# Attention with routed experts on one core: the steps ahead of the first expert in a new order, its first token block copied alone, more dummy products

## The chip, the cores and the metric

The kernel runs on one core of a Trainium2 chip. The metric is the device time of one execution in microseconds. The core has five engines with queues of their own: TensorE (PE: matrix products and transposes; its weight loads are listed as PEld), VectorE (DVE), ScalarE (ACT), GpSimd (POOL) and SyncE (SP, which here only issues DMAs). The engines wait for each other by semaphores. Products land in PSUM, everything else lies in SBUF.

## The reference

A causal attention over 8 batches, 12 heads, 448 positions and 64 columns a head is followed by a layer of 8 experts. Each of the 8 x 448 = 3584 tokens has 768 columns; each expert takes at most 80 tokens.

```
x = attention(q, k, v)                      # 3584 tokens x 768
logits = x @ w_gate                         # 8 experts
expert_idx = argmax(logits);  gate_w = softmax(logits)[expert_idx]
for e in range(8):
    tok_idx = tokens whose expert is e, the 80 with the largest gate_w
    h = maximum(x[tok_idx] @ w1[e], 0)      # 768 -> 1024
    out[tok_idx] = gate_w[tok_idx] * (h @ w2[e])   # 1024 -> 768
```

Rows of `out` that no expert took are zero.

## The kernel before, in words

**Attention** runs over the batches and, in each, over six pairs of heads. A plan in slots says which piece of which step is issued when. After the attention of a batch its tokens are written to the buffer `xs` in device memory, and a table of the 80 best tokens of every expert is brought up to date: tokens of the batch are compared with each other and with those already in the table.

**The tail** is this work for the last batch. Nothing is left to hide it in, so its order is written out by hand in the string `TAIL` (L43 to L48). Every word is a step; `tc.manual_schedule()` (L974) keeps the steps in this order on every engine. The words that matter here:

- `r0` to `r7`: the eight groups of rows of the last batch (two groups of columns times four blocks of tokens). `w` is the turn on TensorE (three transposes, `rt`, L592), `e` takes it out of PSUM and `m` multiplies by the softmax's norm. `ROW_ENGINES` (L49) names who does it: `v` is one VectorE instruction; `a` is six ScalarE multiplications (L605); `p` is one ScalarE copy (L607) at `e` and a GpSimd multiplication (L619) at `m`. Each group ends with a store to `xs`, issued by SP (L615).
- `r0t r0c`, `r1t r1c`: the one-hot rows and the weights are transposed (`selt`, L731) and copied to `ex` by ScalarE (L734). `hold` is a GpSimd copy (L721) behind which `r1t` is issued.
- `rl lt cp ro`: products of the old table's row with the new tokens (`rl`, L761), comparisons on VectorE (`lt`, L767), counts on TensorE (`cp`, L774) and new ranks on VectorE (`ro`, L779). `places` and `places_more` turn the ranks into two halves of a one-hot table (`rm`, L794).
- `c3w c3l` to `c0w c0l`: the tokens of the batch against each other, a product `rn` (L745) and a VectorE comparison `less` (L748) for each block; `gt3` to `gt0` add them up on TensorE (L813).
- `own rank rr tn tab`: the ranks become a table (`tn`, L857, L860) and the table becomes the list of tokens `idx` (L910, L915).
- `*n`: n dummy products of 448 columns (`keep_warm`, L1096 to L1100), whose result nobody reads.

**The experts.** `gather` (L1183) reads an expert's 80 rows of `xs` by an indirect DMA that GpSimd issues. `inputs` (L1194) turns them (`xtp`, L1204) into six blocks of 128 columns and copies these out of PSUM: a float16 part `xh` on ScalarE (L1208) and the rest `xl` on VectorE (L1209). The weights are loaded in pieces of 1.5 MB and split the same way into `wh` (ScalarE, L1172) and `wl` (VectorE, L1157); a product is then three float16 products (L1230 to L1233). Some weight blocks are not split: `whole` (L1133) names blocks 3 to 5 of the first matrix of expert 0, block 5 of that of experts 1 to 5, and one of the second matrix. For these the tokens are copied in float32 as `xw` (L1207), and the product is one float32 product (L1223), which the profile lists as two passes. Expert 0 begins with its three whole blocks (L1341).

In this part only TensorE's order is fixed by hand (L1334). The program gives ScalarE eight weight splits (three blocks of expert 0 and five of expert 1) ahead of the first `xw`; splits of VectorE are issued behind the list of tokens, and later ones behind `xl`, with `issue_after` (L1156). Layer 1 of an expert is followed by layer 2 of the one before.

Of the kernel before, what the change touches and what calls it, by code (L numbers as in the profile page):

```python
# [7 lines left out]
F32 = mybir.dt.float32  # L8
# [4 lines left out]
AF = mybir.ActivationFunctionType  # L13
ALU = mybir.AluOpType
# [3 lines left out]
P = 128  # L18
# [23 lines left out]

TAIL = """  # L43
u ta ya tb yb v0 td yd tc yc v1 vy guard invert last_rows w gp0 wy close piece gp1 gs
r0w r0e r1w lp r1e r1m r2w r2e rest rest r3w r3e lg logit shifted chosen rest rest r4w r4e r5w *2
sums one_hot wsum one_zero wmore columns r0t r0c *2 weight weighted parts hold r1t r1c rl r3m r4m r5e r5m r6w r6e r6m
lt c3w c3l cp c2w r7w r7e r7m ro c2l c1w gt3 *1 c0w c1l gt2 *1 c0l *1 gt1 places *1 earlier gt0 places_more own *3 rank rr tn tab *17
"""  # L48
ROW_ENGINES = "vpappppp"  # L49


@with_exitstack
def attention_then_moe(
# [12 lines left out]
    nc = tc.nc  # L66
# [7 lines left out]
    NC1 = D // P  # L74
# [12 lines left out]
    ps_m = ctx.enter_context(tc.tile_pool(name="ps_m", bufs=2, space=PSUM))  # L87
# [30 lines left out]
    SL = max(2, min(P, CAP))  # L118
# [65 lines left out]
    wmore = [wearly]  # L184
# [19 lines left out]
    def piece_parts():  # L204

        got = []
        k = PIECES[len(wload)][3]
        got.append(piece())
        half = PW // k // 2

        def part(j, x):
            t, src = got[0]
            nc.sync.dma_start(t[:, j, x * half:(x + 1) * half], src[:, j, x * half:(x + 1) * half])
        return [lambda j=j, x=x: part(j, x) for j in range(k) for x in range(2)]
# [7 lines left out]
    lg = keep.tile([P, NT, H * E], F32, name="lg")  # L222
# [717 lines left out]
    n = len(pairs)  # L940
# [33 lines left out]
    with tc.manual_schedule():  # L974
# [14 lines left out]
            out=nowhere, out_offset=None, in_=w2.rearrange("e p c (g d) -> (e p c g) d", d=DH)[0:N, :],  # L989
# [10 lines left out]
        deferred, parts = [], []  # L1000
        for i, pr in enumerate(pairs):
# [8 lines left out]
            h = i // PH  # L1010
# [12 lines left out]
            for k in range(SLOTS):  # L1023
# [24 lines left out]
                if i > 4 and k % 4 == 3:  # L1048
                    if not parts and len(wload) < WBUF:
                        parts = piece_parts()  # L1050
# [10 lines left out]
        rest = [f for k in sorted(plan) for f in plan.pop(k)]  # L1061
# [34 lines left out]
        def keep_warm(times):  # L1096

            wp = ps_v.tile([P, S], F32, name="wp", tag="xp")
            for _ in range(times):
                nc.tensor.matmul(wp, identb, before[:, 0:S], start=True, stop=True)  # L1100
        for i, x in enumerate(ROW_ENGINES):
            g, t = divmod(i, NT)
# [25 lines left out]
    ps = ctx.enter_context(tc.tile_pool(name="ps", bufs=2, space=PSUM, reuse_waits="tile"))  # L1128
# [4 lines left out]
    def whole(e, which, c):  # L1133

        if e >= E - 2:
            return False
        return c == NC2 - 1 if which == 2 else c >= (NC1 // 2 if e == 0 else NC1 - 1)

    SW, SX = 32.0, 8.0
# [3 lines left out]
    PER = NC1 if NC1 * SL <= 512 else NC1 // 2  # L1143
# [50 lines left out]
    def inputs(u):  # L1194

        h = ffn.tile([P, NC1, SL], F16, name="xh", tag="xh")
        l = ffn.tile([P, NC1, SL], F16, name="xl", tag="xl")
        nw = sum(whole(u.e, 1, c) for c in range(NC1))
        w = ffn.tile([P, NC1 // 2, SL], F32, name="xw", tag="xw", bufs=1)
        per = NC1 // 2 if u.e == 0 else PER  # L1200
        for c0 in reversed(range(0, NC1, per)):
            tp = ps_m.tile([P, per, SL], F32, name="xtp", tag="misc", padded_shape=[P, PER, SL])
            for c in range(per):
                nc.tensor.transpose(tp[:, c, :], u.xg[:, (c0 + c) * P:(c0 + c + 1) * P], ident[0:SL, 0:SL])  # L1204
            part = slice(c0, c0 + per)
            if nw and c0 + per == NC1:
                nc.scalar.activation(w[:, NC1 // 2 - nw:], tp[:, per - nw:], AF.Copy, scale=SX * SW)  # L1207
            nc.scalar.activation(h[:, part], tp, AF.Copy, scale=SX)  # L1208
            u.xl = nc.vector.scalar_tensor_tensor(out=l[:, part], in0=tp, scalar=SX, in1=h[:, part], op0=ALU.mult,  # L1209
                                                  op1=ALU.subtract)  # L1210
        u.x = h, l, w

    def product(u, a, which, x, n, outs, per, blocks=None):
# [104 lines left out]
    for s in range(NSL):  # L1318
# [4 lines left out]
        for e in range(E):  # L1323
            u = Unit()
# [9 lines left out]
        with tc.manual_schedule(engines={mybir.EngineType.PE}):  # L1334
            for e in range(E + 1):
                if e < E:
                    u = units[e]
                    if e == 0:

                        order, lows = split_pieces(n1)  # L1340
                        u.order = order[NC1 // 2:] + order[:NC1 // 2]  # L1341
                        units[1].order, more = split_pieces(n1)
                        for nx in units[1:AHEAD]:
                            gather(nx)
                        for _, f in lows:
                            low_after.append(f())
                        inputs(u)
                        low_after.append(u.xl)
                        for _, f in more:
                            f()  # L1350
                    elif e > 1:
                        u.order = split_now(n1)
                    if e + AHEAD < E:
                        gather(units[e + AHEAD])

                    def between(p=prev, nx=units[e + 1] if e + 1 < E else None):
                        if p and p.e:
                            outputs(units[p.e - 1])
                        elif nx and not p:
                            inputs(nx)  # L1360
                    if prev:
                        hidden(prev)
                    layer1(u, between)
                if prev:
                    prev.order = split_now(n2)
                    if e == E:
                        hidden(prev)

                    between = None
                    if e + 1 < E:  # L1370
                        between = lambda u=units[e + 1]: inputs(u)
                    elif e == E and prev.e:
                        between = lambda u=units[prev.e - 1]: outputs(u)
                    layer2(prev, between)
                    if e == E:
                        outputs(prev)
# [38 lines left out]
```

## Time and profile before

| | |
|---|---|
| timed runs, median of 3 | 472.5 us (471.6 to 473.13) |
| profiled execution | 476.79 us |
| its span (first to last instruction) | 474.9 us |
| TensorE, VectorE, ScalarE, GpSimd busy | 442.5, 414.9, 397.6, 317.1 us |
| mean granted clock of TensorE | 0.988 |
| read and written | 253 GB/s over the span |
| tail of the last batch | about 330 to 348 us of the span |
| first gather issued | 348.34 us |
| last instruction of the experts on VectorE | 469.0 us |

All times of single instructions count from the start of the span. A row of the timeline gives start, length, engine, line, operation, output and inputs, shape, count, and in brackets how long the engine had stood idle before it and what ended that. A row of a stretch gives busy time and count of each engine in it, then the clock that TensorE was granted, the share of the DMA engines that were busy, and GB/s. Instructions of one engine can overlap by a little, since the next one starts before the last has written its end.

### The profile page before, as it was taken

The page shows a single profiled execution, that of the slowest core. Times are in us where ns is not written, and L with a number is a line of the kernel's source. Part 1 is how long each engine was busy: PE and PEld are TensorE (multiplying, and loading weights), DVE is VectorE, ACT ScalarE, POOL GpSimd, SP SyncE. Part 2 cuts the span into 40 slices and gives each one's busy share as a digit, 9 for nine tenths or more (in the row PEclk, how much of TensorE's full clock was granted, in tenths as well). Part 3 has the DMA queues.
Part 4 walks back from the last instruction along what each step waited for, and adds up shares of the span by engine and source line. Part 5 has one row for each costly group of instructions (what it writes and reads, how often), then busy time and mean ns, then how long its engine had stood idle before and what let it go on. Part 6 is the DMA issues. An engine that isn't in the chain of part 4 may idle for free.

```text
span 474.9 us, 14808 instructions
## 1 busy us (share of the span) xinstructions
PE 442.5 (93%) x5279; PEld 347.1 (73%) x5279; DVE 414.9 (87%) x1272; ACT 397.6 (84%) x1076; POOL 317.1 (67%) x382
## 2 busy tenths in 40 slices
PE   4899999999999999999999999999889999989894
PEld 2566677767767776776677668666569998988894
DVE  6788799988988999998899899996786999999982
ACT  6898989979988897998898889787593989988892
POOL 7999999988998996997898799720440265500101
PEclk9999999999999999999999999999996999999999
DMA  7858999899779569687956947469849999999801
GB/s 211 185 151 233 277 310 243 258 285 258 212 220 296 165 211 303 167 244 219 310 156 215 304 154 226 146 213 385 343 155 344 355 397 383 392 425 424 338 24 43
DMA packets 43001, 120.88 MB, mean 255 GB/s; under 512 B 6146, under 2 KB 23810, under 8 KB 39472
## 3 DMA queue, kind: packets, MB, share of 16 engines
q1 hardware_dynamic: 41712, 116.21, 75.7%
q0 software_dynamic: 1056, 3.51, 2.3%
q8 instruction: 41, 0.67, 0.6%
q10 hardware_dynamic: 160, 0.23, 0.2%
q14 instruction: 32, 0.26, 0.2%
HBM read 96.36 MB, written 23.99 MB: 253 GB/s over the span
## 4 chain that ended last, share of the span: by engine, by line
PE 77%; DMA 9%; DVE 7%; issue 3%; POOL 2%; SPq 1%; ACT 0%; POOLq 0%; ACTq 0%; DVEq 0%
PE xp L495 15%; PE tp L465 14%; PE sp L423 6%; DMA qk<-k_t 6%; PE sp L424 5%; PE rt L592 4%; PE hp L1223 4%; PE sp L433 3%; PE hp L1232 3%; PE hp L1233 3%; PE hp L1230 3%; PE gp L545 3%; PE op L1233 2%; PE op L1232 2%; PE op L1230 2%
## 5 line engine op out<-in xcount | busy, mean ns | idle before, releaser
L448 ACT ACTIVATE prob<-ns,nb 128x128 f32<-128x128 f32 (+3 forms) x336 | 177.2, 529 | 24.9 <-DVE nb L445 23.2
L445 DVE CUSTOM_DVE_ANT_0 ns<-sp,mask 128x384 f32<-128x384 f32 (+2 forms) x288 | 115.4, 413 | 17.9 <-PE sp L424 12.1
L465 PE MATMUL tp<-ident,prob 128*128 128x128 f32 x768 | 118.9, 277 | 1.4 <-ACT prob L448 1.2
L477 ACT COPY PT<-tp 128x512 f32<-128x512 f32 x182 | 104.0, 572 | 16.5 <-PE sp L423 7.9
L395 POOL TENSOR_TENSOR qk<-qk,qk 128x448 f16<-128x448 f32 x92 | 98.3, 1091 | 11.9 <-DVE qk L387 6.8
L1157 DVE SCALAR_TENSOR_TENSOR wl<-wraw,wh 128x768 f16<-128x768 f32 (+1 forms) x98 | 98.1, 1059 | 3.3 <-ACT wh L1172 2.2
L465 PEld LDWEIGHTS tp<-ident,prob 128*128 128x128 f32 x768 | 89.8, 142 | 13.3 <-ACT prob L448 3.3
L495 PE MATMUL xp<-PT,vt 128*64 128x448 f32 (+3 forms) x768 | 91.1, 380 | 0.0
L1172 ACT ACTIVATE wh<-wraw 128x768 f16<-128x768 f32 (+1 forms) x98 | 84.7, 926 | 3.7 <-PE hp L1233 1.2
L423 PE MATMUL sp<-qk 128*128 128x384 f16 (+2 forms) x288 | 75.9, 279 | 12.4 <-DVE nb L445 6.9
L495 PEld LDWEIGHTS xp<-PT,vt 128*64 128x64 f32 x768 | 53.8, 137 | 42.7 <-issue 22.6
L424 PE MATMUL sp<-qk 128*128 128x384 f16 (+2 forms) x288 | 78.0, 277 | 1.3 <-POOL qk L349 0.5
L1233 PEld LDWEIGHTS <-wl 128*128 128x128 f16 x668 | 67.1, 100 | 3.0 <-issue 1.5
L1232 PEld LDWEIGHTS <-wh 128*128 128x128 f16 x668 | 67.1, 100 | 2.7 <-issue 2.6
L1230 PEld LDWEIGHTS <-wh 128*128 128x128 f16 x668 | 67.6, 101 | 0.6 <-issue 0.6
L1311 POOL DMA_INDIRECT out<-yo,idx x8 | 22.4, 2802 | 66.6 <-ACT yo L1308 63.4
L448 ACT ACTIVATION_READ_ACCUMULATOR prob<-ns,nb 128x1 f32 x336 | 63.9, 190 | 0.0
L390 POOL TENSOR_TENSOR qk<-qk,qk 64x448 f16<-64x448 f32 x46 | 53.4, 1160 | 3.4
L391 POOL TENSOR_TENSOR qk<-qk,qk 64x448 f16<-64x448 f32 x46 | 51.4, 1117 | 3.2
L387 DVE CAST qk<-qk 128x896 f16<-128x896 f32 x46 | 40.0, 869 | 2.2 <-DMA qk<-k_t 2.1
L384 POOL CAST qk<-qk 64x896 f16<-64x896 f32 x40 | 38.5, 962 | 3.8 <-PE sp L436 2.5
L423 PEld LDWEIGHTS <-qk 128*128 128x128 f16 x288 | 28.5, 99 | 15.7 <-issue 7.3
(188 smaller groups left out, 905.9 us busy)
## 6 DMA issues: line engine op xcount, KB each, us to landing
wraw<-w SPq DMA_DIRECT2D x27, 1536.0 KB, 10.9
qk<-k_t SPq DMA_DIRECT2D x92, 224.0 KB, 6.0
out<-mask_l SPq DMA_DIRECT2D x56, 192.0 KB, 4.4
qk<-q_t SPq DMA_DIRECT2D x23, 448.0 KB, 4.0
vt<-v_t SPq DMA_DIRECT2D x24, 384.0 KB, 5.7
xs<-xr SPq DMA_DIRECT2D x42, 192.0 KB, 3.1
wraw<-w SPq DMA_DIRECT2D x24, 256.0 KB, 5.7
vt<-v_t SPq DMA_DIRECT2D x24, 64.0 KB, 5.2
```

Of the source, the lines that this page charges most:

```text
L395: nc.gpsimd.tensor_tensor(out=k_lo[j][:, i], in0=kf[j][:, i], in1=k_hi[j][:, i], op=ALU.subtract)
L423: nc.tensor.matmul(sp[:, 0:w], qx[:, p, t * P:w], kx[:, p, 0:w], start=True, stop=False)
L424: nc.tensor.matmul(sp[:, 0:w], qx[:, p, t * P:w], lx[:, p, 0:w], start=False, stop=True)
L445: pr.masked = nc.vector.tensor_tensor_reduce(out=ns[:, 0:w], in0=sp[:, 0:w], in1=m, scale=-1.0 / 8.0, scalar=HUGE, op0=ALU.add, op1=ALU.mi ...
L448: nc.scalar.activation(pr.P[:, off:off + w], ns[:, 0:w], AF.Exp, bias=nb, scale=-1.0, accum_out=total)
L465: nc.tensor.transpose(pr.tp[:, i], pr.P[:, off:off + P], ident)
L477: copy(dst, src)
L495: state["pe"] = nc.tensor.matmul(xp[rows, 0:w], st["vt"][:, c, p * P + j * DH:p * P + (j + 1) * DH], pr.PT[:, j, n0:n0 + w], start=(c == 0 ...
L1157: return nc.vector.scalar_tensor_tensor(out=l, in0=src, scalar=SW, in1=h, op0=ALU.mult, op1=ALU.subtract)
L1230: nc.tensor.matmul(o, wh[:, ws], ah[:, c, :], start=(x == 0 and i % per == 0), stop=False, skip_group_check=True)
L1232: nc.tensor.matmul(o, wh[:, ws], al[:, c, :], start=False, stop=False, skip_group_check=True)
L1233: nc.tensor.matmul(o, wl[:, ws], ah[:, c, :], start=False, stop=(x == n - 1), skip_group_check=True)
```

## The change

Three places are edited.

1. `TAIL`: `rl` stands ahead of `r1t`, and `lt cp ro places` stand ahead of `c3w c3l`, where `places` stood far behind. The row groups are spread anew: `r2m` and `r3m` stand earlier, `r4e`, `r4m`, `r5w` and `r5e` later. There are six more dummy products: 34 instead of 28, three of them in the last group, behind `tab` (20 instead of 17), and two ahead of `rank` (5 instead of 3).
2. `ROW_ENGINES`: row group 2 goes from `a` to `p`, row group 5 from `p` to `a`.
3. `inputs`: a block that is only used whole is no longer split into `xh` and `xl` as well. For expert 0 the six blocks are turned and copied in three parts: block 3 alone, in a PSUM tile of its own from the pool of the outputs (`ps`, tag `o`), then blocks 4 and 5, then blocks 0 to 2. Before, it was two parts of three blocks. For experts 1 to 5 `xh` and `xl` have five blocks instead of six.

```
-r0w r0e r1w lp r1e r1m r2w r2e rest rest r3w r3e lg logit shifted chosen rest rest r4w r4e r5w *2
-sums one_hot wsum one_zero wmore columns r0t r0c *2 weight weighted parts hold r1t r1c rl r3m r4m r5e r5m r6w r6e r6m
-lt c3w c3l cp c2w r7w r7e r7m ro c2l c1w gt3 *1 c0w c1l gt2 *1 c0l *1 gt1 places *1 earlier gt0 places_more own *3 rank rr tn tab *17
+r0w r0e r1w lp r1e r1m rest rest r2w r2e r2m r3w lg logit shifted r3e chosen rest rest r4w *1
+sums one_hot wsum one_zero wmore r3m columns r0t r0c *3 weight weighted parts hold rl r1t r1c *1 lt cp ro places r5w
+c3w c3l r4e r4m r5e r6w r6e r6m c2w r7w r7e r7m c2l c1w gt3 *2 c0w c1l gt2 *1 c0l gt1 *1 places_more earlier gt0
+own *5 rank rr tn tab *20
 """
-ROW_ENGINES = "vpappppp"
+ROW_ENGINES = "vppppapp"
...
-        nw = sum(whole(u.e, 1, c) for c in range(NC1))
         w = ffn.tile([P, NC1 // 2, SL], F32, name="xw", tag="xw", bufs=1)
-        per = NC1 // 2 if u.e == 0 else PER
-        for c0 in reversed(range(0, NC1, per)):
-            tp = ps_m.tile([P, per, SL], F32, name="xtp", tag="misc", padded_shape=[P, PER, SL])
-            for c in range(per):
+        parts = [(0, NC1)] if u.e else [(NC1 // 2, NC1 // 2 + 1), (NC1 // 2 + 1, NC1), (0, NC1 // 2)]
+        for i, (c0, c1) in enumerate(parts):
+            n = c1 - c0
+            if i == 0 and len(parts) > 1:
+                tp = ps.tile([P, n, SL], F32, name="xtp", tag="o", padded_shape=[P, PER, SL])
+            else:
+                tp = ps_m.tile([P, n, SL], F32, name="xtp", tag="misc", padded_shape=[P, PER, SL])
+            for c in range(n):
                 nc.tensor.transpose(tp[:, c, :], u.xg[:, (c0 + c) * P:(c0 + c + 1) * P], ident[0:SL, 0:SL])
-            part = slice(c0, c0 + per)
-            if nw and c0 + per == NC1:
-                nc.scalar.activation(w[:, NC1 // 2 - nw:], tp[:, per - nw:], AF.Copy, scale=SX * SW)
-            nc.scalar.activation(h[:, part], tp, AF.Copy, scale=SX)
-            u.xl = nc.vector.scalar_tensor_tensor(out=l[:, part], in0=tp, scalar=SX, in1=h[:, part], op0=ALU.mult,
-                                                  op1=ALU.subtract)
+            split = [c for c in range(c0, c1) if not whole(u.e, 1, c)]
+            m = len(split)
+            assert split == list(range(c0, c0 + m))
+            if m < n:
+                nc.scalar.activation(w[:, c0 + m - NC1 // 2:c1 - NC1 // 2], tp[:, m:], AF.Copy, scale=SX * SW)
+            if m:
+                nc.scalar.activation(h[:, c0:c0 + m], tp[:, 0:m], AF.Copy, scale=SX)
+                u.xl = nc.vector.scalar_tensor_tensor(out=l[:, c0:c0 + m], in0=tp[:, 0:m], scalar=SX, in1=h[:, c0:c0 + m],
+                                                      op0=ALU.mult, op1=ALU.subtract)
```

## The prediction

> **What bounds the kernel now.** I read the page first: its span, the forty slices, and the shares of the chain that ended last.
>
> ```profile
> span 474.9 us, 14808 instructions
> PE   4899999999999999999999999999889999989894
> PEclk9999999999999999999999999999996999999999
> PE 77%; DMA 9%; DVE 7%; issue 3%; POOL 2%; SPq 1%; ACT 0%; POOLq 0%; ACTq 0%; DVEq 0%
> ```
>
> TensorE carries the chain, and one slice of forty, the thirty-first, has a clock below full. This slice (356 to 368 us) is where the expert stage begins, just behind the code that the change edits. So I asked next for the chain from the gather on, and for busy times there.
>
> ```profile
> 348.34 3.17 DMA xg<-xs,idx
> 351.55 0.44 PE xtp L1204 x3
> 352.50 9.25 PE hp L1223 x48
> 361.75 0.80 PE xtp L1204 x6
> 370.24 1.82 PE hp L1223 x16
> ```
> ```profile
> 353.93:364.17 10.24, 10.24 (x72) 10.24 (x71) 6.06 (x7) 2.66 (x5) 1.24 (x2) 0.50 0.98 348
> 367.00:430.00 63.00, 59.98 (x1285) 59.04 (x1282) 62.65 (x73) 58.02 (x90) 24.74 (x7) 1.00 1.00 392
> ```
> ```profile
> 363.37 0.66 DVE L1209 SCALAR_TENSOR_TENSOR xl<-xtp,xh 128x480 f16<-128x480 f32 x1 [4.18 <-ACT xh L1208]
> ```
>
> The order is: gather lands (351.5), three transposes, a copy, then 48 float32 passes (the 24 products of the three raw weight blocks) that take 9.25 us. Sixteen such passes take 1.82 us later, at full clock, so 48 would take 5.46. The difference, 3.8 us, is the clock: 0.50 from 353.93 to 364.17. While that lasts, the copies of unit 1 cannot start, and VectorE stands still for 4.18 us. From 367 to 430 us VectorE is busy 62.65 of 63 us and the DMA engines all of it. A microsecond that the start of the expert stage gains or loses is therefore handed on to the end, as long as both of them shift with it.
>
> What makes the clock fall? The cold stretch is 10.24 us, three times 3.41. I cut the trace into such pieces, counted back from 353.93, and took PE busy time (first four rows) and the dummy products alone (last two).
>
> ```profile
> 343.69:347.10 3.41, 2.67 (x27) 1.00 0.61 203
> 350.52:353.93 3.41, 2.43 (x21) 1.00 0.56 137
> 357.35:360.76 3.41, 3.41 (x18) 0.50 1.01 275
> 360.76:364.17 3.41, 3.41 (x39) 0.50 0.99 385
> ```
> ```profile
> 343.69:347.10 3.41, 2.12 (x7) 0.60 (x7) 1.00 0.61 203
> 350.52:353.93 3.41, 0.36 (x2) 0.00 (x0) 1.00 0.56 137
> ```
>
> Busy time does not sort them: a piece that is busy throughout stays cold. Moved columns do. The piece ahead of the fall has one dummy product's 448 columns that begins in it and 19 transposes and passes of 80: 1968. The piece from 343.69, with seven dummy products (3136), was followed by full clock; 18 passes of 80 (1440) did not bring it back, 39 instructions of 80 (3120) did. So one bound between 1968 and 3120 columns a piece would explain all four. A piece of float32 passes alone at full clock holds 3.41 / 0.114 = 30 of them, 2400 columns: in between, and open.
>
> The Trainium skill ("TensorE: Matmul & The Clock Gate", Part 1) gives such a free-running window, 3413 ns, and the trace agrees with 10.24. Its section "Why this matters for your kernels" asks only that idle gaps stay under about 3 us; by that the clock would not fall here and extra dummy products would be worth nothing. The trace has no such gap and the clock fell.
>
> **The times.** The profiled execution took 476.79 us for its span of 474.9; the three timed runs have a median of 472.5 (471.6 to 473.13). The profiled one is 4.3 us above it. The cold stretch costs about as much (below), so the timed runs may lack it; or profiling costs this much. I cannot tell, and it decides the rivals. I sum differences against 476.79 and take them over to 472.5.
>
> **The change, part by part.**
>
> *Products with the old table first.*
>
> ```profile
> 340.54 0.57 ACT L734 COPY ex<-selt 24x512 bf16<-24x512 bf16 x1 [0.50 <-PE selt L731]
> 341.06 0.21 POOL L721 COPY held<-grest 128x1 f32<-128x1 f32 x1 [0.72 <-DVE grest L715]
> 341.37 0.38 PE L731 MATMUL selt<-identb,mv 128*128 128x128 bf16 x4 [0.49 <-POOL held L721]
> 341.59 0.31 PE L761 MATMUL rl<-row,ex 128*128 128x80 bf16 x4
> 341.94 0.30 DVE L767 TENSOR_SCALAR_CACHE_REDUCE lt<-rl,ggw 128x80 bf16<-128x80 f32 x1 [0.71 <-PE rl L761]
> 342.61 0.29 DVE L767 TENSOR_SCALAR_CACHE_REDUCE lt<-rl,ggw 128x80 bf16<-128x80 f32 x1
> 342.63 0.53 PE L774 MATMUL cp<-oh,lt 128*80 128x8 bf16 x4
> 342.83 0.75 DVE L748 SCALAR_TENSOR_TENSOR less<-rn,ggw,before 128x512 bf16<-128x512 f32 x1
> 343.51 0.21 DVE L779 TENSOR_SCALAR ro<-cp,pnum 80x8 f16<-80x8 f32 x1
> ```
>
> Now `rl` stands behind the transposes that wait for `held`. Its own operand is there when the copy ends, 341.11; ahead of them it starts near 341.17 instead of 341.59, and the comparisons `lt` move 0.42 us forward. They end at 342.48 instead of 342.90. Then a new wait: `ro` and `places` now come straight behind `lt`, while before the comparison `less` filled the time that `cp` takes. The last `cp` product ended at 343.16, 0.26 behind `lt`; with the hand-over, VectorE idles 0.3. Queued behind `cp` on TensorE are r5w and the first `rn`; `places` hides them on VectorE. Net -0.1; bounds -0.42 (no new wait) and +0.2 (`rn` late behind r5w).
>
> *Row groups spread anew.* Row group 2 turns from six multiplications on ScalarE to a copy and a GpSimd multiply, group 5 the other way, and group 4's copy moves behind the weights' rows.
>
> ```profile
> 337.50 1.34 ACT L605 ACTIVATE xrl<-rt,sums 128x64 f32<-128x64 f32 x6 [0.17 <-PE rt L592]
> 342.27 0.84 ACT L607 COPY xrl<-rt 128x384 f32<-128x384 f32 x2
> 343.71 0.47 ACT L607 COPY xrl<-rt 64x384 f32<-64x384 f32 x1 [0.60 <-PE rt L592]
> 344.09 7.68 ACT L1172 ACTIVATE wh<-wraw 128x1024 f16<-128x1024 f32 x8
> 352.07 0.37 ACT L1207 ACTIVATE xw<-xtp 128x240 f32<-128x240 f32 x1 [0.31 <-PE xtp L1204]
> ```
>
> At 337.5 the saving of 0.9 us falls where ScalarE has room: nothing. Behind 342.3 it costs. Group 4's copy takes 0.42 (half of 0.84) and ends at 342.8; group 5's turns stand behind `cp` and are done by about 343.15; its six multiplications take 1.34, to 344.5; groups 6 and 7 add 0.42 and 0.47: 345.35 instead of 344.18. The eight weight splits (7.68 us) follow, and `xw` behind them, in program order. They ended 0.30 us before `xw` began; pushed by 1.2 us they hold `xw` up by 0.9. If the build lets `xw` pass the last split, it is nothing. Bounds 0 and +0.9; neither is nearer, so I take the middle, +0.45.
>
> ```profile
> 344.39 0.82 POOL L619 TENSOR_TENSOR xrl<-xrl,rql 64x384 f32<-64x384 f32 x1
> 345.24 0.45 SPq L615 DMA_DIRECT2D xs<-xrl  x1
> xs<-xrl SPq DMA_DIRECT2D x6, 192.0 KB, 1.8
> ```
>
> The last rows' GpSimd multiply ended at 345.21 and their store, last in SP's queue, landed near 347.0, 1.3 us before the gather of 348.34. With group 6 copied at 344.9, GpSimd ends at 346.6 and the store lands near 348.4: the cover of 1.3 is just used up. I take 0; gone, it costs 0.2 to 0.5.
>
> *First block alone, raw blocks without halves.*
>
> ```profile
> 352.34 0.63 ACT L1208 ACTIVATE xh<-xtp 128x240 f16<-128x240 f32 x2
> 352.79 0.72 DVE L1209 SCALAR_TENSOR_TENSOR xl<-xtp,xh 128x240 f16<-128x240 f32 x2 [0.68 <-ACT xh L1208]
> 362.64 0.24 ACT L1207 ACTIVATE xw<-xtp 128x80 f32<-128x80 f32 x1 [6.75 <-PE xtp L1204]
> ```
>
> The first pass waits for a copy of 80 columns (0.24) instead of 240 (0.37): -0.13; bounds -0.25 (two transposes less to wait for, too) and 0. One `xh` and one `xl` of unit 0 go, on engines that wait for TensorE's 9.25 us afterwards: nothing now, -0.36 if that cover goes. In units 1 to 5 `xl` falls from 480 columns to 400, 0.66 / 6 = 0.11 each, in the stretch where VectorE is full: -0.55 at most, 0 if the DMA, full as well, decides; I take -0.4, since VectorE had waits of its own nowhere there.
>
> *Six more dummy products.*
>
> ```profile
> 347.50 3.38 PE L1100 MATMUL wp<-before,identb 128*128 128x448 bf16 x17
> ```
>
> One takes 3.38 / 17 = 0.2 us. Three lie behind the table: 20 last until 351.5, when the gather lands at 351.5: nothing, up to +0.2. The others fill waits of TensorE: nothing.
>
> The sum: -0.1 + 0.45 - 0.13 - 0.4 = -0.2, with the clock as it is: 476.6 for the profiled execution, **472.3** on the scale of the median. The bounds together give 471.3 to 473.8.
>
> **Rivals.**
>
> *The clock holds (chance 0.33).* The three products add up to 1344 columns to the piece ahead of the fall: 1968 becomes up to 3312, above 3120. For it: that. Against it: the next piece is float32 alone, 2400 columns, undecided; and the timed runs may be warm already. Worth: TensorE gets back 3.8 us and 1.0 of the float16 work that ran at half clock until 364.17, but VectorE only its idle 4.18: 472.3 - 4.2 = 468.1. If the fall is merely one piece later, 3.41 / 2 = 1.7 us: 470.6.
>
> *ScalarE's queue delays the passes (0.20), slower.* The splits hold `xw` the whole 0.9 us; the passes begin at 353.1 instead of 352.5, and the gap behind the dummy products is 1.6 us again, as from 350.9 to 352.5 now. With pieces as in the trace the float16 work begins 0.6 us later, so the piece that ended at 364.17 has some nine of its float16 instructions less (28 in 2.0 us) and three float32 passes more: 33 times 80, 2640 columns. If the bound lies above that, the clock stays low for one piece more, 1.7 us: 472.3 + 0.45 + 1.7 = 474.4. Timed runs that were warm and turn cold would lose 4.2: 476.5. For it: ScalarE had only 0.30 us of slack. Against: 2640 is itself undecided, and so is the build's order.
>
> *Last rows late (0.05).* The gather waits for the store: 472.3 + 0.5 = 472.8, still the same.
>
> **How the numbers follow.** A measurement of this kernel tells about 0.3%, 1.4 us, from no change. The forecast has 0.42 and lies within it, but for 0.04 at its lower end; so faster 0.33 + 0.04 = 0.37, slower 0.20 + 0.02 for an unseen wait = 0.22, same 0.41. The range goes from the held clock, 468.1, to the delayed passes, 474.4; 0.15 lies above or below. The likeliest case alone spans 471.3 to 473.8.
>
> **What would show it.** Right: `lt` starts 0.4 us sooner behind `oh`, with an idle of 0.3 before `ro`; the eight splits begin near 345.3; `xl` has 400 columns and takes 0.55. The clock row tells the rest: three cold pieces again (forecast), none (first rival), or `xw` waiting for a split (second). Wrong would be a start of `xw` right behind its transpose with the clock low all the same and a time off by more than 1.4 us: then something later in the expert stage has moved.

## The result and the profile after

The changed kernel takes 479.43 us (median of 4, 477.38 to 480.26), the kernel before 472.05 (median of 4, 471.09 to 473.13): ratio 1.0144, interval 1.012 to 1.0168. It is **7.4 us slower**. The forecast was 472.3 with a range of 468.1 to 474.4, so the time lies outside it, on the other side of no change.

First the scale. The profiled execution of the changed kernel is one of the four timed ones (480.26 us, span 478.4). The profiled execution of before that the prediction was built on, 476.79, was one in which the clock had fallen. The unchanged kernel was therefore profiled anew (`b_same`, below: 473.54 us, span 471.7, clock 0.998 against 0.988); with its clock up it lies within 1.1 us of the median of its ten executions, so profiling does not cost 4 us. That profile, not the first one, is what stands for the kernel before from here on.

The page of the changed kernel looks like the one of before, with one cold slice:

```profile
PEclk9999999999999999999999999999996999999999
```

The timeline shows more. Here are the changed kernel's rows from the tail's row sums to the second unit's transposes:

```profile
338.99 0.83 POOL L620 TENSOR_TENSOR xrl<-xrl,sums 128x384 f32<-128x384 f32 x1 [0.31 <-ACT xrl L608]
339.07 0.80 DVE L642 TENSOR_TENSOR gsh<-logit,gmx 128x32 f32<-128x32 f32 x1
339.77 0.82 POOL L620 TENSOR_TENSOR xrl<-xrl,rql 64x384 f32<-64x384 f32 x1
339.90 0.75 DVE L649 SCALAR_TENSOR_TENSOR goh<-gsh,dec 128x32 f32<-128x32 f32 x1
344.37 0.22 DVE L780 TENSOR_SCALAR ro<-cp,pnum 80x8 f16<-80x8 f32 x1 [0.29 <-PE cp L775]
344.39 0.83 POOL L620 TENSOR_TENSOR xrl<-xrl,sums 128x384 f32<-128x384 f32 x1 [1.54 <-ACT xrl L608]
344.62 0.94 DVE L795 TENSOR_TENSOR rm<-ro,slots_e 80x320 bf16<-80x320 f16 x1
347.32 0.82 POOL L620 TENSOR_TENSOR xrl<-xrl,rql 64x384 f32<-64x384 f32 x1
347.38 1.12 DVE L795 TENSOR_TENSOR rm<-ro,slots_e 80x320 bf16<-80x320 f16 x1
350.43 0.16 DVE L916 TENSOR_TENSOR idx<-xf,tn 80x8 int32<-80x8 f32 x1
351.10 3.50 DVE L1158 SCALAR_TENSOR_TENSOR wl<-wraw,wh 128x1024 f16<-128x1024 f32 x3
351.23 2.04 POOL L1190 DMA_INDIRECT xg<-xs,idx  x1 [3.09 <-DVE gws L924]
353.58 1.85 POOL L1190 DMA_INDIRECT xg<-xs,idx  x1 [0.31 <-issue]
350.04 3.94 PE L1101 MATMUL wp<-before,identb 128*128 128x448 bf16 x20
355.32 0.61 PE L1208 MATMUL xtp<-ident,xg 80*128 80x80 f32 x6 [1.34 <-DMA xg<-xs,idx]
355.91 9.52 PE L1230 MATMUL hp<-xw,wraw 128*128 128x80 f32 x48
365.22 1.01 PE L1208 MATMUL xtp<-ident,xg 80*128 80x80 f32 x6
```

And the same steps of the kernel before, profiled anew with its clock up:

```profile
339.64 0.19 DVE L641 TENSOR_TENSOR gsh<-logit,gmx 128x32 f32<-128x32 f32 x1
339.87 0.19 DVE L648 SCALAR_TENSOR_TENSOR goh<-gsh,dec 128x32 f32<-128x32 f32 x1
345.41 0.82 POOL L619 TENSOR_TENSOR xrl<-xrl,rql 64x384 f32<-64x384 f32 x1
345.88 0.70 DVE L794 TENSOR_TENSOR rm<-ro,slots_e 80x320 bf16<-80x320 f16 x1
346.77 0.48 DVE L794 TENSOR_TENSOR rm<-ro,slots_e 80x320 bf16<-80x320 f16 x1
348.53 3.38 PE L1100 MATMUL wp<-before,identb 128*128 128x448 bf16 x17
348.91 0.16 DVE L915 TENSOR_TENSOR idx<-xf,tn 80x8 int32<-80x8 f32 x1
349.36 1.08 POOL L1189 DMA_INDIRECT xg<-xs,idx  x1 [3.13 <-DVE gws L922]
349.58 3.56 DVE L1157 SCALAR_TENSOR_TENSOR wl<-wraw,wh 128x1024 f16<-128x1024 f32 x3
350.75 0.96 POOL L1189 DMA_INDIRECT xg<-xs,idx  x1 [0.30 <-issue]
352.30 0.64 PE L1204 MATMUL xtp<-ident,xg 80*128 80x80 f32 x6 [0.40 <-DMA xg<-xs,idx]
353.25 5.58 PE L1223 MATMUL hp<-xw,wraw 128*128 128x80 f32 x48 [0.31 <-ACT xw L1207]
358.67 0.58 PE L1204 MATMUL xtp<-ident,xg 80*128 80x80 f32 x6
```

Profiles differ by up to 1.5 us in where the tail begins, so the two are compared from one instruction that no edit precedes, the copy `gs` of the last batch (337.02 before, 336.44 after). All later tables count from it.

| | before | after | later by |
|---|---|---|---|
| list of tokens `idx` done | 12.05 | 14.15 | 2.10 |
| first gather starts behind the list | 0.29 | 0.65 | 0.36 |
| GpSimd's part of that gather | 1.08 | 2.04 | 0.96 |
| first transposes start | 15.28 | 18.89 | 3.61, of it 0.19 new |
| float32 passes start | 16.23 | 19.47 | 3.24, so 0.37 regained |
| second transposes start | 21.65 | 28.79 | 7.14, of it 3.90 new |
| last instruction starts | 134.63 | 141.96 | 7.33 |

The loss is complete when the second unit's transposes begin, and from there to the end of these two profiles nothing is made good and 0.2 us are added. The experiments ask for its parts: why the list is late, why the gather is doubled, and why the passes take 9.52 us instead of 5.58. (The expectations below count the passes to shortly behind the start of the last one, and say 9.2 and 5.4.)

The theory: GpSimd's row multiplications, moved to new places, stand in the way of VectorE's instructions and make the list late (A1); the last row's store now comes so late that the gather waits for it and no longer for the list (A2) and falls behind VectorE's first weight split, which stands in GpSimd's way (A3); the gap on TensorE grows past what keeps the clock up (A4). The rivals: the new copies in `inputs` (B); the new order of the products or the added dummy products (C); ScalarE's queue, as the prediction had it (D).

### The profile page after: what moved, and what is told of

It reads as the page before. It is cut to its first block, busy times and chain, and to the rows that moved or that the text cites. A ratio compares the mean times of both kernels' runs of the same rounds, so it can differ in the third digit from the quotient of the medians.

```text
span 478.4 us, 14819 instructions
## 1 busy us (share of the span) xinstructions
PE 444.9 (93%) x5285; PEld 347.9 (73%) x5285; DVE 416.4 (87%) x1271; ACT 397.6 (83%) x1076; POOL 315.9 (66%) x382
## 4 chain that ended last, share of the span: by engine, by line
PE 79%; DVE 5%; DMA 5%; POOL 5%; issue 4%; SPq 1%; POOLq 0%; ACT 0%; DVEq 0%; ACTq 0%
PE tp L466 15%; PE xp L496 15%; PE sp L424 6%; PE sp L425 5%; PE hp L1230 4%; PE rt L593 4%; DMA qk<-k_t 3%; PE sp L434 3%; PE hp L1237 3%; PE hp L1240 3%; PE op L1240 3%; PE hp L1239 3%; PE op L1239 3%; PE gp L546 2%; PE op L1237 2%
## 5 line engine op out<-in xcount | busy, mean ns | idle before, releaser
L1318 POOL DMA_INDIRECT out<-yo,idx x8 | 20.0, 2501 | 67.3 <-ACT yo L1315 64.1
```

## The experiments

**The kernel before again, and each half of the change** (`b_same`: no edit; `b_tail`: before with the new `TAIL` and `ROW_ENGINES`; `b_inputs`: before with the new `inputs`).

> The kernel before, unchanged, to see the granted clock of its timed executions and not only of the profiled one. Theory A (two-state clock): most of its timed executions hold the full clock through the 48 float32 passes, their time is about 472 us with a mean clock of 0.994 or more, and an execution whose clock falls takes about 476.5 us at about 0.988. Rival B (the profiled execution was only slow by chance, the cold stretch is in all of them): executions at 472 us have the same mean clock of about 0.988 as the profiled one.

> The kernel before with the new order of the tail and the new engines of the row groups alone, blocks copied as before. Theory A (GpSimd's multiplies hold up VectorE in the tail, the late start then lets the clock fall): all of the loss, 479 to 480 us, mean clock about 0.987, the subtraction gsh and the comparison goh 0.75 to 0.8 us instead of 0.2. Rival C (the loss comes from the copies of the first block and the new PSUM tile): about 472 us.

> The kernel before with the new copies of the token blocks alone, the tail as before. Theory A: 471 to 472.5 us, the clock as in the kernel before, xl of units 1 to 5 at 0.56 us. Rival C: 476 to 480 us.

| | this, us | before, us | ratio |
|---|---|---|---|
| b_same | 472.49 | 472.74 | 0.9994 [0.9971, 1.0016] |
| b_tail | 479.68 | 472.74 | 1.0153 [1.0114, 1.0192] |
| b_inputs | 472.62 | 472.74 | 1.0003 [0.9982, 1.0023] |

The whole loss is in the tail's order; rival B is out. In `b_same` and the runs of before beside it, 5 of 29 executions had a mean clock of 0.989 or less, the others up to 0.999: the kernel before usually keeps its clock. These are rows of `b_tail`:

```profile
350.02 0.16 DVE L916 TENSOR_TENSOR idx<-xf,tn 80x8 int32<-80x8 f32 x1
350.69 3.50 DVE L1158 SCALAR_TENSOR_TENSOR wl<-wraw,wh 128x1024 f16<-128x1024 f32 x3
351.23 1.64 POOL L1190 DMA_INDIRECT xg<-xs,idx  x1 [3.08 <-DVE gws L924]
355.74 5.58 PE L1224 MATMUL hp<-xw,wraw 128*128 128x80 f32 x48 [0.25 <-ACT xw L1208]
363.64 0.61 PE L1205 MATMUL xtp<-ident,xg 80*128 80x80 f32 x6 [2.31 <-DMA xg<-xs,idx]
```

Two things are to be seen. The clock held here (5.58 us of passes), and the second transposes were late all the same, because TensorE waited 2.31 us for the second gather. And the first gather starts 1.05 behind the list, 0.56 after `gws` (to 350.67), which the row names as its releaser. What came last is the row store: its last packet ended 0.29 before the list was done, its semaphore was complete 0.35 behind that packet, and it took another 0.75 on GpSimd's queue until GpSimd went on, 1.10 behind the packet in all. In the changed kernel the packet ended 0.69 before the list, and GpSimd went on 1.11 behind it, 0.42 behind the list. In before it ended 1.09 before the list and GpSimd went on 0.04 behind the list: the cover was nearly used up already.

**Two of the early multiplications moved behind `hold`** (`a_mults_late`, from after).

```
-... r2w r2e r2m r3w ... r3m columns ... hold rl r1t
+... r2w r2e r3w ... columns ... hold r2m r3m rl r1t
```

> The changed kernel with the GpSimd multiplies of row groups 2 and 3 moved behind the hold, where group 3's stood before. Theory A: gsh and goh fall back to 0.2 us each, the list of tokens is done 1.2 us sooner, and if the first pass comes early enough for the clock to hold in some executions, the time falls from 479.4 to between 474 and 478 us. Rival D (ScalarE's row work behind the weights' rows is the cause, not the multiplies): no change, 479 us or more, since ScalarE and the stores of the rows are not sooner.

Measured 477.81 against 472.74, ratio 1.0101 [1.005, 1.0152]. `gsh` and `goh` take 0.19 each again and the list is done at 12.99 instead of 14.15: the collision was worth 1.16 there. `rm` still takes 0.95 and 1.11, and the gather still starts 0.65 behind the list and takes 2.03. So A1 is right for the list, and is a part only. What it is worth at the end is not shown: the medians differ by 1.6 us, but the four executions (476.0 to 480.4) overlap those of after.

**The row groups as before, all else as after** (`a_rows_before`).

```
-r0w r0e r1w lp r1e r1m rest rest r2w r2e r2m r3w lg logit shifted r3e chosen rest rest r4w *1
-... wmore r3m columns ... rl r1t r1c *1 lt cp ro places r5w
-c3w c3l r4e r4m r5e r6w r6e r6m c2w r7w r7e r7m c2l ...
-ROW_ENGINES = "vppppapp"
+r0w r0e r1w lp r1e r1m r2w r2e rest rest r3w r3e lg logit shifted chosen rest rest r4w r4e r5w *1
+... wmore columns ... rl r1t r1c *1 r3m r4m r5e r5m lt cp r6w r6e r6m ro places
+c3w c3l c2w r7w r7e r7m c2l ...
+ROW_ENGINES = "vpappppp"
```

> The changed kernel with the row groups and their engines placed as before; products with the old table first, first block alone and 34 dummy products stay. Theory A (the spread of the row groups is the whole loss: GpSimd's multiplies hold up VectorE's two-tensor operations by 2 us, and the late last store makes the gathers start behind the first weight remainders wl): list of tokens 0.1 to 0.4 us sooner than in the kernel before, gather 0.3 us behind it, 471.5 to 473 us. Rival E (the new order of products, or the dummy products, cost by themselves): 475 us or more.

Measured 474.34 against 472.49, ratio 1.0048 [1.0032, 1.0065]: some 5 of the 7.4 us are gone. The list is done at 12.37, the gather starts 0.29 behind it and takes 1.08, TensorE's gap between the last dummy product and the first pass is 0.76, the passes take 5.58. What remains, 1.9 us by the medians, is above what was expected. The profiled execution is the fastest of the four (472.54; the others took 474.2 to 474.5), so the trace does not hold what the others lost.

**The weight splits held back until the second gather is issued** (`a_lows_late`, from after; `a_rows_lows` is this and the row groups as before).

```
+second = gather(nx)
+token = const.tile([P, 2], F32, name="token")
+with tc.issue_after(second.ins):
+    nc.gpsimd.memset(token[:, 0:1], 0.0)
+low_after.append(nc.vector.tensor_copy(token[:, 1:2], token[:, 0:1]))
```

> The changed kernel with VectorE's weight remainders wl held until GpSimd has issued the second gather. Theory A: the list of tokens is as late as in the changed kernel, but each of the first two gathers takes 1.0 us on GpSimd instead of 2.0 and 1.85, the first transposes come 1 us sooner, the second gather is ahead of the weights' DMA and TensorE no longer waits for it behind the float32 passes: 475.5 to 477.5 us. Rival F (the gathers are slow for another reason, such as the stores or the descriptors themselves): the gathers keep their 2 us, 479 to 481 us.

> Both: row groups as before, wl held until the second gather is issued, the rest of the change kept. Theory A: like the row groups as before alone, or up to 1 us better since the first three gathers no longer meet wl: 470.5 to 472.5 us. Rival F: as without the hold, or slower by the 2 us for which VectorE's remainders are held.

`a_lows_late`: 475.71 against 472.49, ratio 1.0083 [1.0065, 1.0101]. `a_rows_lows`: 473.24, ratio 1.0008 [0.9985, 1.0032], above its forecast too and not told apart from before. Of `a_lows_late`:

```profile
350.10 0.16 DVE L916 TENSOR_TENSOR idx<-xf,tn 80x8 int32<-80x8 f32 x1
351.30 1.08 POOL L1190 DMA_INDIRECT xg<-xs,idx  x1 [3.08 <-DVE gws L924]
352.69 0.96 POOL L1190 DMA_INDIRECT xg<-xs,idx  x1 [0.31 <-issue]
353.91 3.57 DVE L1158 SCALAR_TENSOR_TENSOR wl<-wraw,wh 128x1024 f16<-128x1024 f32 x3
355.17 5.58 PE L1230 MATMUL hp<-xw,wraw 128*128 128x80 f32 x48
360.59 0.58 PE L1208 MATMUL xtp<-ident,xg 80*128 80x80 f32 x6
```

With the list as late as in after and the wait for the store even longer (the gather starts 1.04 behind the list), but the split out of the way, the gather takes 1.08 again. TensorE's gap is 1.51 and the clock holds; the second transposes begin at 24.83 instead of 28.79. Half of the loss, 3.7 us by the medians, hangs on who comes first, gather or split (A3), with what follows from it.

**The last store in three thirds** (`b_store_split`, before; the same columns in three DMAs: the store takes longer to issue, nothing else is late).

```
+if ps_x and g == 1 and t == NT - 1:
+    w = NH * P // 3
+    for i in range(3):
+        nc.sync.dma_start(..., xr[0:m, i * w:(i + 1) * w])
+    return
```

> The kernel before with the last row group's store issued as three stores of a third of the columns each, so that the last of them is issued about 0.65 us later; nothing else. Theory A (the gather waits for the last store, which is just in time in the kernel before; once it is late, the gather starts behind the first wl and takes twice as long, and the second falls behind the weights' DMA): gather starts 0.5 to 1.0 us behind the list instead of 0.29, takes 1.6 to 2.0 us, the first float32 pass comes 1.2 to 1.4 us later, time 474 to 476.5 us. Rival G (a late store costs what it is late by): 473 to 473.4 us, not to be told from the kernel before.

Measured 478.34 against 472.49, ratio 1.0126 [1.0107, 1.0144]: more than expected, nearly the loss of the whole change, from one DMA. Its rows:

```profile
348.63 0.16 DVE L921 TENSOR_TENSOR idx<-xf,tn 80x8 int32<-80x8 f32 x1
349.30 3.50 DVE L1163 SCALAR_TENSOR_TENSOR wl<-wraw,wh 128x1024 f16<-128x1024 f32 x3
350.11 1.37 POOL L1195 DMA_INDIRECT xg<-xs,idx  x1 [4.15 <-DVE gws L929]
354.57 10.53 PE L1229 MATMUL hp<-xw,wraw 128*128 128x80 f32 x48 [0.24 <-ACT xw L1213]
```

The list is done at 12.05, as in before. The store's last packet ends at 11.92 instead of 10.96, and the gather starts 1.02 later than in before. The transposes are late by 1.60, the gap is 2.95, the clock falls, and the passes take 10.53 instead of 5.58. This is A2 to A4 without A1.

**More or fewer dummy products** (`b_few_dummies`: 8 instead of 17 behind `tab`; `b_split_warm`: the split store with 26; `a_more_warm`: after with 26 instead of 20; `b_split_both`: `b_split_warm` with the hold of `a_lows_late`).

```
-rank rr tn tab *17
+rank rr tn tab *8
```

> The kernel before with 8 dummy products instead of 17 behind the table, so that TensorE stands idle for about 3.1 us instead of 1.3 ahead of the first float32 pass; nothing else moves. Theory A (the clock falls where this gap is over about 1.7 us, and a fall costs about 4 us): mean clock 0.978 to 0.989 in all executions, the 48 passes take 9 to 10.5 us instead of 5.4, 475.5 to 477 us. Rival H (a slow clock there is made good later, where VectorE and the DMA decide): at most 474 us.

> The kernel before with the last store in three parts, as in the run before, and 26 dummy products instead of 17 behind the table, so that the gap ahead of the first float32 pass is 1.2 us again. Theory A: the clock holds in most executions, the passes take 5.4 us; the second gather, behind the weights' DMA, still lands near 25.3 us behind the start of gs, so the second block of transposes starts there instead of at 28.15: 475 to 476.5 us against 478.3. Rival I (the clock falls for another reason than the gap): still 478 us, clock 0.98.

> The changed kernel with 26 dummy products instead of 20 behind the table; they end about when the first gather lands. Theory A: the clock holds in most executions, the passes take 5.4 us instead of 9.2, the second transposes then wait for the second gather until about 27.4 us behind gs (28.8 now): 477 to 478.5 us against 479.4. Rival I: no change, clock 0.98 to 0.989.

> As the one before, and VectorE's remainders wl are held until the second gather is issued. Theory A: all that is left is the late store itself, about 1 us: gathers of 1.0 us each, the second gather ahead of the weights' DMA, passes of 5.4 us, second transposes at 22.6 to 23 us behind gs, 473 to 474.5 us. If the gathers and the clock do not account for the rest of the 5.8 us, it stays above 475.

| | this, us | before, us | ratio | passes, us | second transposes at |
|---|---|---|---|---|---|
| b_few_dummies | 477.57 | 472.37 | 1.011 [1.0082, 1.0139] | 10.53 | 27.00 |
| b_split_warm | 474.46 | 472.37 | 1.0042 [1.0027, 1.0058] | 5.58 | 24.40 |
| b_split_both | 474.8 | 472.37 | 1.004 [1.0021, 1.0059] | 5.58 | 23.00 |
| a_more_warm | 479.79 | 472.37 | 1.0149 [1.0116, 1.0183] | 5.58 | 28.57 |

`b_few_dummies` leaves list and gather as they are and only lengthens TensorE's gap, to 3.5 (3.1 was expected): the clock alone costs 5.2 us, 0.6 more than the forecast allowed. `b_split_warm` takes 3.9 of the split store's loss back and ends 0.5 below its forecast. `b_split_both` is a miss: the hold brings the second transposes 1.4 forward, and the end gains nothing. And `a_more_warm` is a miss that says most. Its rows:

```profile
354.33 1.85 POOL L1190 DMA_INDIRECT xg<-xs,idx  x1 [0.31 <-issue]
356.76 5.58 PE L1230 MATMUL hp<-xw,wraw 128*128 128x80 f32 x48
365.04 0.60 PE L1208 MATMUL xtp<-ident,xg 80*128 80x80 f32 x6 [2.69 <-DMA xg<-xs,idx]
```

The passes are warm, and TensorE then stands still until the second gather lands. That gather's GpSimd part took 1.85 instead of 0.96 and ended at 356.18, behind the issue of the next weight piece (355.37); it landed over 8 us later. In before it ended at 351.71, ahead of that issue (353.17), and no wait shows. (In this execution the list was also done 0.72 later, 14.87, so its time isn't all due to the edit.) So in after the fallen clock and the late second gather cover each other: the gather lands at 27.75 and the cold passes let the second transposes begin at 28.79. Curing the clock alone can gain 1 us there at most, and gained nothing; curing the second gather alone was not tried. The cover is not whole in every case: of the four executions of `b_tail` two had a mean clock of 0.991 and 0.992 (477.77 and 478.46 us) and two one of 0.976 and 0.979 (481.28 and 480.91).

**The remaining parts alone** (all from before; `b_mults_early`: group 2 on GpSimd, `r2m` and `r3m` early; `b_products`: the new order of products and `places`; `b_dummies`: 34 dummy products; `b_copies_20`: the new `inputs` with 20 dummy products behind `tab`).

```
b_mults_early:
-... r1m r2w r2e rest rest ... wmore columns ... r1c rl r3m r4m ...
-ROW_ENGINES = "vpappppp"
+... r1m r2w r2e r2m rest rest ... wmore r3m columns ... r1c rl r4m ...
+ROW_ENGINES = "vppppppp"
b_products:
-... hold r1t r1c rl r3m r4m r5e r5m r6w r6e r6m
-lt c3w c3l cp c2w r7w r7e r7m ro c2l ... gt1 places *1 earlier gt0 places_more ...
+... hold rl r1t r1c r3m r4m r5e r5m lt cp r6w r6e r6m ro places
+c3w c3l c2w r7w r7e r7m c2l ... gt1 *1 places_more earlier gt0 ...
```

> The kernel before with row group 2 on GpSimd and the multiplies of groups 2 and 3 ahead of columns, as in the changed kernel; all else as before, so that the last store is not later than the list. Theory A (the collision on its own costs what it takes, once the stores and gathers keep their places): gsh and goh 0.75 to 0.8 us each, the list 1.0 to 1.3 us later, gathers of 1.0 us that start 0.29 behind it, clock held: 473.2 to 474.2 us. Rival J (any late list brings the whole loss): 477 us or more.

> The kernel before with the new order of products alone (old table's products first, places ahead of the new tokens' comparisons), the row groups, dummy products and copies as before. Theory K (this is what leaves 1.9 us when the row groups are put back): the list 0.3 us later than before, 473.5 to 474.5 us. Theory L (the 1.9 us are chance or the dummy products): 472 to 473 us.

> The kernel before with the 34 dummy products of the changed kernel alone. Theory K: 471.5 to 472.7 us, the clock held more often. Theory L with the dummy products as the cause: 473.5 to 474.5 us.

> A version meant to be faster than both: the kernel before with the new copies of the token blocks and 20 dummy products behind the table, so that the gap ahead of the first float32 pass is 0.65 us instead of 1.24. The clock should hold in all executions and not in three of four; since a fall costs up to 4 us, 0.3 to 1 us are to be had: 471.5 to 472.3 us. If falls in the kernel before are rarer than the clocks make it look, no change.

| | this, us | before, us | ratio | list done at |
|---|---|---|---|---|
| b_mults_early | 473.28 | 472.43 | 1.0023 [0.9996, 1.0049] | 12.84 |
| b_products | 473.28 | 472.43 | 1.0018 [0.9995, 1.0042] | 12.50 |
| b_dummies | 472.38 | 472.43 | 0.9992 [0.9975, 1.0009] | 12.11 |
| b_copies_20 | 472.0 | 472.43 | 0.9985 [0.9966, 1.0003] | 12.05 |

`b_mults_early` makes the list 0.79 later, less than expected, since only one of the two collisions is whole:

```profile
338.98 0.44 DVE L641 TENSOR_TENSOR gsh<-logit,gmx 128x32 f32<-128x32 f32 x1
339.46 0.75 DVE L648 SCALAR_TENSOR_TENSOR goh<-gsh,dec 128x32 f32<-128x32 f32 x1
```

But here the last rows' store ends in time, the gather starts 0.29 behind the list and ahead of the split, and the time is 0.2% off, not told apart from before. A list that is 0.8 late does not bring the whole loss; what it costs by itself lies between -0.2 and 2.3 us (0.85 by the medians). Rival C is small: the products' order makes the list 0.44 later (`rm` takes 0.94 beside a GpSimd multiplication, and VectorE idles 0.29 ahead of `ro`), though its 473.28 lies between the two theories; the dummy products change nothing that shows. `b_copies_20`, the parts of the change that cost nothing, cannot be told from before either: no gain shows in them.

## Why the prediction was wrong, point by point

**The order of the products**: `lt` 0.42 earlier and an idle of 0.3 before `ro`, both as worked out (5.94 to 5.52 in `a_rows_before`; the 0.29 in the row of `ro`). The net of -0.1 missed `rm`: moved up, its first half meets a GpSimd multiplication sooner after that has begun (in before it met one as well, from 345.41), and 0.70 turns into 0.94. With the row groups as before the list was 0.31 later than before, not 0.1 earlier.

**"At 337.5 the saving of 0.9 us falls where ScalarE has room: nothing"** is the step that failed first. It counted the instruction that left ScalarE and not the one that came to GpSimd. This one runs from 338.99 to 339.82, and VectorE's `gsh`, 0.19 alone, starts at 339.07 and ends at 339.87; the next runs from 339.77 to 340.59, and `goh` ends at 340.65. Each time VectorE's instruction ends 0.05 to 0.06 behind GpSimd's. Together 1.17 on the path to the list; the second half of `rm` loses 0.64 beside the last rows' multiplication. With `rm`'s first half (0.24) and the idle of 0.29, less 0.42, that makes 1.92 of the 2.10 by which the list is late.

The Trainium skill ("SBUF — State Buffer", sections "Who interferes with whom" and "SBUF: two separate sides") says that a VectorE instruction with two inputs in SBUF contends with a GpSimd instruction that reads SBUF, and that the one that comes second blocks until the first has ended. The ends of `gsh` and `goh`, 0.05 and 0.06 behind GpSimd's, agree; the page would have spoken against this change.

**"Last rows late"**, "I take 0; gone, it costs 0.2 to 0.5", was a rival with a chance of 0.05. It is the step that carries most of the loss: `b_store_split`, which makes this store alone late, costs 5.9 us. Its mechanism came true, and both its numbers were wrong. The prediction saw a cover of 1.3 us between landing and gather; in fact GpSimd goes on only 1.1 us behind the last packet, so the slack was nearly nil. And it priced the wait alone (0.36 measured), not what stands behind it: the split that the gather had been ahead of by 0.22 us (349.36 and 349.58). Behind it, the gather's GpSimd part takes 2.04, the second one 1.85 and falls behind a weight piece, and the gap on TensorE grows from 1.35 to 1.93.

**The clock.** The prediction could not tell whether its profile was typical, and summed from it. It wasn't: a fallen clock is the exception in before and the rule in after (mean clock 0.982 to 0.989 in all four executions). "The clock holds", chance 0.33, was for the most part already so in before, and could bring little; `b_copies_20`, meant to hold it always, shows no gain that its interval could tell. The sentence "timed runs that were warm and turn cold would lose 4.2" had the right size: 5.2 in `b_few_dummies`, 3.9 between `b_store_split` and `b_split_warm`. The picture of pieces of 3.41 us stood up. In after the clock is low for 10.24 us, three pieces, again:

```profile
357.05:367.29 10.24, 10.24 (x65) 10.24 (x65) 5.77 (x6) 2.85 (x6) 2.55 (x2) 0.50 1.02 341
```

The count of moved columns did not stand up. The pieces lie on one grid through a whole trace, so others can be counted. Here are a piece of `b_split_warm` and the one behind it, then the same for `b_tail`:

```profile
357.17:360.59 3.42, 2.69 (x25) 2.54 (x23) 3.42 (x4) 0.50 (x1) 0.00 (x0) 1.00 1.01 288
360.59:364.00 3.41, 3.02 (x78) 3.05 (x79) 1.97 (x4) 2.23 (x4) 0.96 (x1) 1.00 1.04 365
```
```profile
361.81:365.22 3.41, 1.58 (x38) 1.61 (x39) 0.78 (x2) 0.70 (x2) 0.71 (x1) 1.00 1.03 321
365.22:368.64 3.42, 3.42 (x57) 3.42 (x54) 3.07 (x5) 2.48 (x4) 0.25 (x1) 0.50 0.98 413
```

All instructions of the two counted pieces have 80 columns. Behind the 25 of the first, at most 2000 columns, the clock held; behind the 38 of the second, 3040 columns, it fell. So no one bound between 1968 and 3120 sorts the pieces. Busy time does not either: the clock fell behind 2.43 us of it (from 350.52 in the prediction's profile) and held behind 1.62 (from 339.99 in after). (The prediction's 18 and 39 instructions are those that overlap a piece; 16 and 37 begin in it.) The 25 are float32 passes, and most of the 38 are float16 products. As an estimate made afterwards from all eighteen traces, with each instruction's columns counted by its share inside the piece and those of float32 products twice, the clock fell behind pieces of at most 3130 columns and held behind pieces of at least 2770; no run tried that this is the cause.

By the gap between the last dummy product and the first pass, the profiles sort so: up to 1.5 us the clock held through the passes, at 2.95 and 3.5 it fell, and in between it went either way (it fell at 1.62 and 1.93, and held at 1.67, 1.72 and 2.16).

**ScalarE's queue** (the slower rival, 0.20) is out. The row work did end later on ScalarE, the splits `wh` starting at 10.24 instead of 8.09, but `xw` waited for TensorE and not for them:

```profile
346.68 7.71 ACT L1173 ACTIVATE wh<-wraw 128x1024 f16<-128x1024 f32 x8
355.62 0.44 ACT L1213 ACTIVATE xw<-xtp 128x80 f32<-128x80 f32 x2 [1.24 <-PE xtp L1208]
366.99 0.58 DVE L1216 SCALAR_TENSOR_TENSOR xl<-xtp,xh 128x400 f16<-128x400 f32 x1 [4.47 <-ACT xh L1215]
```

The last split had ended at 354.39. The third row belongs to the **copies**: 400 columns in 0.58 instead of 480 in 0.66, 0.08 of the expected 0.11, and the first pass comes 0.37 sooner behind the transposes, more than the 0.13 forecast. In `b_inputs` neither shows at the end (1.0003), though its interval of about 1 us either way would not tell the 0.5 that was forecast for both.

**The sign of being wrong** that the prediction named did come: `xw` starts straight behind its transposes with the clock low, and the time is off by far more than 1.4 us. It was read ahead of time as "something later in the expert stage has moved". What moved stands ahead of that: the list, the last store and the first two gathers.

**What stays open.** From the second transposes on, a delay passes to the end about one to one, as the prediction said (7.14 and 7.33 in after; 5.35 and 5.06 in `b_few_dummies`), but with exceptions of over 1 us either way: `b_split_warm` is 2.75 late there and 1.28 at the end of its profile, `a_rows_lows` 0.37 and 2.14. What the clock goes by is open too. The 1.9 us that remain in `a_rows_before` are explained by the list only to 0.3, and the single parts add up to under 1; four executions may not be enough to say more.

## What to carry to other kernels

When an instruction moves to another engine, cost it on the engine that receives it, and look for what runs beside it there: here VectorE's instructions with two inputs in SBUF waited for GpSimd's multiplications, and GpSimd's gather for one of VectorE's. A slack between a DMA's landing and its waiter counts from where the waiter really goes on, not from the last packet, and the price of using it up is set by what stands next in line on the other engines. Before a sum is made from a profile, ask whether the profiled execution's time is that of the timed runs; where it is 4 us off, the difference is the first thing to explain.

## What the runs showed of the hardware that was not expected

- **A gather behind a VectorE split waits for the split to end.** A split takes 1.22 us; the gather's GpSimd part takes 0.96 to 1.08 alone. The first gather, begun inside a split, ended 0.96 behind that split's end: the split starts at 351.10 in after, so 351.10 + 1.22 + 0.96 = 353.28, measured 351.23 + 2.04 = 353.27; in `b_tail` 350.69 gives 352.87, measured 352.87; in `b_store_split` 349.30 gives 351.48, measured 351.48. Begun 0.22 ahead of a split it took 1.08, and the split lost nothing. Second gathers that began inside a split ended 0.83 behind its end; but in before the second gather begins 0.02 behind a split's start and takes 0.96 all the same. That the order is the cause is shown by `a_lows_late`, where the split comes later and the gather takes 1.08.
- **GpSimd goes on 1.1 us behind a store's last packet** (1.10 in `b_tail`, 1.11 in after). Only 0.35 of it passes until the store's semaphore is complete; the rest passes on GpSimd's own queue. The row of the gather names another releaser for this wait.
- **Two delays can cover each other**: in after, cold passes hold the second transposes until 28.79 and the second gather lands only at 27.75, so dummy products alone gain nothing there (`a_more_warm`), while in `b_split_warm` they gain 3.9 us.
